# Attention and expert routing on one core: a pair's scores and its transposes each in one block, values in the scores' ring of PSUM tiles

## The chip, the cores and the metric

The kernel runs on one core of one Trainium2 chip. Its time is the device time of one execution in microseconds (us); the median of several runs counts. TensorE multiplies matrices into PSUM (8 banks), VectorE and ScalarE read PSUM, GpSimd issues the indirect DMAs, and SyncE issues all other DMAs.

## The reference

Causal attention over 4 batches of 12 heads (448 tokens, head dimension 64) gives 1792 rows of 768. They go through a layer of 8 experts. Routing is greedy over all pairs of token and expert in order of their logit, with at most 224 tokens for each expert; every token then passes through its expert's two matrices.

```python
scores = scale * np.matmul(q, k.transpose(0, 1, 3, 2))
scores = np.where(mask, -1e9, scores)
scores = scores - np.max(scores, axis=-1, keepdims=True)
attn = np.exp(scores)
attn = attn / (np.sum(attn, axis=-1, keepdims=True) + 1e-09)
x = np.matmul(attn, v)                 # rows of 12 heads x 64
...
flat = (x @ w_gate).flatten()
order = np.argsort(-flat)
for idx in order:
    tok, e = (int(idx) // E, int(idx) % E)
    if assigned[tok] >= 0 or counts[e] >= cap:
        continue
    assigned[tok] = e
    counts[e] += 1
...
for e in range(E):
    mask = assigned == e
    out[mask] = np.maximum(x[mask] @ w1[e], 0.0) @ w2[e]
```

## The kernel before

**Attention.** The 48 heads go in 24 pairs. A pair's two heads lie on partitions 0 to 63 and 64 to 127, so their score matmuls run side by side on two halves of TensorE's rows. The 448 queries are four blocks of 112; block i needs only the first 112 (i + 1) keys. `scores` (line 210) computes the blocks in sets, each set with a tile for each head: set (3,) has 448 columns, set (2, 0) has 336 + 112, set (1,) has 224. `mask` (VectorE) adds the causal mask, copies to SBUF and finds the row maximum; `exp` (ScalarE) exponentiates and sums. `transp` turns the 10 blocks of a head's probabilities on TensorE, in three groups of 4, 4 and 2, each in a tile; `keep_pt` copies each group to SBUF on ScalarE or VectorE. `av` multiplies by the values, with the two heads on two halves of TensorE's columns, and `xt_ev` copies the result (128 x 448, transposed) out. `rows_tr` and `rows_dve` turn it into rows, divide by the sums and put it into `xio`, which `store` writes to DRAM. Every four or two pairs, `logits_mm` and `logits_tr` compute gate logits.

**PSUM.** Three rings of tiles share the 8 banks: `s` (4, scores), `av` (1, values product) and `t` (3, everything else: groups of transposes, row turns, logits, and the last score set of pair 0). A ring hands its tiles out in order; a new user waits for whoever last read the tile.

**Order.** `plan` adds tasks for iterations n = 0 to 26. TensorE's tasks form one chain (`pe`, line 419), so its order is the order in which `plan` adds them; the other engines' orders come from a list scheduler (`Schedule.run`) that picks by priority and by durations written in the code. Among them copies of transposes stand above masks, and masks above exponentials. TensorE's order in an iteration is:

```python
self.score_set(n, (3,))
self.score_set(n, (2, 0))
self.turn(n - 1, 0)          # 10 transposes of one head
self.score_set(n, (1,))
self.turn(n - 1, 1)          # 10 of the other
self.rows_at(n - 3)
self.logits_back(n - 3)
self.values(n - 1)
self.logits(n - 2)
```

`extras` adds VectorE tasks of lowest priority that prepare the routing.

**Late rows.** `rows_at` serves only pairs below `LATE` = 12. The rows of the other pairs are turned later, by `late` (line 936), while the first routing decision runs on VectorE and TensorE. Each late pair is two half-pairs of two query blocks; a half-pair is divided into `xio` either by ScalarE (`rows_act`, four instructions) or by VectorE (`rows_dve`, one instruction). `PIECES` says after which pairs a part of `xio` is stored. Where TensorE has nothing to do in this stage, `filler` issues matmuls whose result nobody reads. The first gather of tokens (`gather`) needs the routing's list `idx` and all stores (`touch`, a small GpSimd write). Then the eight experts follow, each with its weights split in two parts.

Of the kernel before, what the change touches and what calls it, by code (L numbers as in the profile page):

```python
# [27 lines left out]
QO = (0, 112, 336, 672)  # L28
LATE = 12
PIECES = {14: 3, 17: 3, 20: 3, 22: 2, 23: 1}  # L30
WARM = 10
# [122 lines left out]
class Attention(Schedule):  # L154
    def __init__(self, ctx, tc, gc, keep, k, qk, vP, wgP, xd, L):
        super().__init__()
        self.tc, self.nc, self.k = tc, tc.nc, k
        self.qk, self.vP, self.xd, self.L = qk, vP, xd, L
        self.gc, self.keep = gc, keep
        self.ld = ctx.enter_context(tc.tile_pool(name="ld", bufs=4))  # L160
        self.wk = ctx.enter_context(tc.tile_pool(name="wk", bufs=4))
        self.cs = ctx.enter_context(tc.tile_pool(name="acs", bufs=1))
        self.ps = ctx.enter_context(tc.tile_pool(name="aps", bufs=1, space=PSUM))
        self.QK, self.V = {}, {}
        self.X, self.RS, self.XT, self.S, self.SM, self.PT, self.AV = {}, {}, {}, {}, {}, {}, {}
# [7 lines left out]
        t = self.ps.tile([C, 512], F32, name="t", bufs=3)  # L173
# [36 lines left out]
    def scores(self, pp, lst):  # L210
        ts = [self.ps.tile([C, 512], F32, name=n, bufs=b) for n, b in (("t", 3) if pp == 0 and 1 in lst else ("s", 4),) * 2]
        o = 0
# [27 lines left out]
    def transp(self, pp, sd, sg):  # L240
        P = self.SM[pp, sd][0]
        t = self.ps.tile([C, 512], F32, name="t", bufs=3)
# [22 lines left out]
    def av(self, pp, js):  # L265
        if 0 in js:
            self.AV[pp] = self.ps.tile([128, S], F32, name="av")
        for j in js:
            for sd in range(2):
                m = S - j * C  # L270
                self.nc.tensor.matmul(self.AV[pp][sd * 64:sd * 64 + 64, j * C:], self.V[2 * pp + sd][:, j, :],  # L271
                                      self.PT[pp, sd][:, KO[j]:KO[j] + m], start=j == 0, stop=j == 2)
# [7 lines left out]
    def xt_ev(self, e, pp):  # L280
        self.copy(e, self.XT[pp], self.AV.pop(pp))

# [14 lines left out]
    def rows_tr(self, pp):  # L297
        self.T[pp] = self.ps.tile([C, 512], F32, name="t", bufs=3)
        self.rows_mm(pp, self.T[pp])
# [16 lines left out]
    def rows_dve(self, pp, t, blocks=range(NC)):  # L316
        x, r = self.xslice(pp)
        s = slice(blocks[0], blocks[-1] + 1)
        self.nc.vector.tensor_tensor(x.rearrange("p i (s d) -> p i s d", s=2)[:, s],
                                     t.rearrange("p (i s d) -> p i s d", i=NC, s=2)[:, s], r[:, s], op=OP.mult)  # L320

# [4 lines left out]
    def logits_mm(self, b, half):  # L326
        p0, m = ((0, 4), (4, 2))[half]
        t = self.ps.tile([128, S], F32, name="t", bufs=3)
        for p in range(m):
# [4 lines left out]
    def logits_direct(self, pp):  # L334
        b, q = divmod(pp, 6)
        if q == 4:
            self.u = self.ps.tile([C, NC, 128], F32, name="t", bufs=3)
        for i in range(NC):
# [8 lines left out]
    def logits_tr(self, b, half):  # L347
        m = (4, 2)[half]
        self.u = self.ps.tile([C, NC, 128], F32, name="t", bufs=3)
        for i in range(NC):  # L350
# [26 lines left out]
    def plan(self, rt):  # L377
# [19 lines left out]
        for n in range(NP + 3):  # L397
            self.score_set(n, (3,))
            self.score_set(n, (2, 0))
            self.turn(n - 1, 0)  # L400
            self.score_set(n, (1,))
            self.turn(n - 1, 1)
            self.rows_at(n - 3)
# [19 lines left out]
    def score_set(self, pp, lst):  # L423
        if not 0 <= pp < NP:
            return
        add, pr = self.add, 5.5 - 0.1 * pp
        m = sum(C * (i + 1) for i in lst)

        def work():
            self.scores(pp, lst)  # L430
            if 1 in lst and pp in self.qfree:
                self.fire(self.qfree[pp])

        bank = "t" if pp == 0 and 1 in lst else "s"
        a = self.pe(m * 4 / 2400.0 + 0.01 * len(lst), work, [self.half0 if pp == 0 and 3 in lst else self.got[pp]] + (self.ring("s", 2) if bank == "s" else []), 1)
        free = []
        for sd in range(2):
            for i in lst:
                early = 0.5 if pp == sd == 0 else 0.0
                d = add("DVE", (0.27, 0.39, 0.51, 0.62)[i], lambda sd=sd, i=i: self.mask(pp, sd, i),  # L440
                        [a] + (self.ring("pt", 4 - sd) if i == 3 else []), pr + 0.25 + early)
                free.append(d)
                self.exps[pp, sd, i] = add("ACT", (0.385, 0.47, 0.56, 0.67)[i], lambda sd=sd, i=i: self.exp(pp, sd, i),
                                           [d], pr + early)
        if bank == "t":
            self.rings["t"] = [free[:1], free[1:]]
        else:
            self.rings.setdefault("s", []).append(free)
        if 1 in lst:
            self.rec[pp] = add("DVE", 0.25, lambda: self.recips(pp),  # L450
                               [self.exps[pp, sd, i] for sd in range(2) for i in range(NC)], pr - 0.3)

    def turn(self, pp, sd):
        if not 0 <= pp < NP:
            return
        pr = 5.5 - 0.1 * pp
        for sg, need in ((0, (3, 2, 1, 0)), (1, (3, 2, 1)), (2, (3, 2))):
            n = (4, 4, 2)[sg]
            a = self.pe(0.097 * n, lambda sg=sg: self.transp(pp, sd, sg),
                        [self.exps[pp, sd, i] for i in need] + self.ring("t", 3))  # L460
            dur = {"DVE": 0.31, "ACT": 0.24} if n == 2 else {"DVE": 0.545, "ACT": 0.43}
            c = self.add("ACT/DVE", dur, lambda e, sg=sg: self.keep_pt(e, pp, sd, sg), [a] + self.ring("av", 2), pr + 0.3)
            self.rings.setdefault("t", []).append([c])
            self.pts[pp, sd, sg] = c
        self.rings.setdefault("pt", []).append([a])

    def values(self, pp):
# [3 lines left out]
        for js, sg in (((0,), 0), ((1, 3), 1), ((2,), 2)):  # L471
# [18 lines left out]
        self.xts[pp] = self.add("ACT/DVE", {"ACT": 0.475, "DVE": 0.56}, ev, [a, self.xts.get(pp - 1)], pr + 0.3)  # L490
        self.rings.setdefault("xt", []).append([self.xts[pp]])

    def rows_at(self, pp):
# [3 lines left out]
        pr = 5.3 - 0.1 * pp  # L497
        t = self.pe(0.43, lambda: self.rows_tr(pp), [self.xts[pp]] + self.ring("t", 3))
        d = self.add("DVE", 0.61, lambda: self.rows_dve(pp, self.T.pop(pp)), [t, self.rec[pp]], pr + 0.3)
# [8 lines left out]
    def logits(self, pp):  # L508
        b, q = divmod(pp, 6)
        if pp in (NP - 2, NP - 1):  # L510
            free = self.ring("t", 3) if q == 4 else []
            self.lts = self.pe(0.4, lambda: self.logits_direct(pp), [self.xts[pp]] + free)
# [3 lines left out]
        if q not in (3, 5) or not 0 <= pp < NP:  # L516
# [4 lines left out]
        t = self.pe(0.77, lambda: self.logits_mm(b, half),  # L521
                    [self.xts[6 * b + p0 + u] for u in range(m)] + self.ring("t", 3), 3)
        c = self.add("ACT/DVE", {"ACT": 0.42, "DVE": 0.56}, lambda e: self.logits_cp(e, b, half), [t], pr + 0.3)
# [3 lines left out]
    def logits_back(self, pp):  # L527
# [8 lines left out]
        else:  # L536
            t = self.pe(0.43, lambda: self.logits_tr(b, half), [self.lts] + self.ring("t", 3))
        d = self.add("DVE", (1.1, 1.05)[half], lambda: self.logits_ev(b, half),
# [12 lines left out]
    def finish(self, rt):  # L551
        rt.early_count(self.G, self.ps.tile([128, S], F32, name="av"))

# [308 lines left out]
class Experts(Schedule):  # L862
# [73 lines left out]
    def late(self):  # L936
        at = self.at
        act, done = {}, []
        for n, pp in enumerate(range(LATE, NP)):
# [322 lines left out]
```

## Time and profile before

| | |
|---|---|
| median of 3 runs | 512.79 us (511.56 to 512.80) |
| the profiled execution | 514.21 us, span 512.3 us from the first to the last instruction |
| granted TensorE clock, mean | 0.999 |
| TensorE, VectorE, ScalarE busy | 496.0, 408.3, 281.6 us |
| pairs (scores to values) | about 6 to 184 us |
| first routing decision with late rows | about 185 to 204 us |
| experts | about 211 us to the end |

The profile is of one execution. Busy time is the sum of an engine's instructions; matmuls overlap, so their durations say less than the distance from one start to the next. A timeline row merges neighbouring instructions of one line and one engine: start, length from the first start to the last end, count, and in brackets the idle time before it and who ended it.

### The profile page before, as it was taken

Reading aid. Unit: us, or ns where it says so; the run is one execution under the profiler, and the core shown is the slowest. Engines: PE = TensorE matmul, PEld = TensorE weight load, DVE = VectorE, ACT = ScalarE, POOL = GpSimd, SP = SyncE. Lnnn points to the kernel's source line nnn. Section 1 sums busy time; section 2 is a strip of 40 time slices with the busy share of each in tenths; the row PEclk is TensorE's granted clock in tenths of the full one; section 3 lists DMA queues with packets and bytes.
Section 4 is the critical chain, followed back from the end, with each engine's and each line's share of the span. In section 5 each row is a group of like instructions: output and inputs, shape, how many; then the busy total and the mean of one; then the engine's idle time right before and its main releaser. Section 6 shows DMA issues by size and latency. Waiting matters only on the chain.

```text
span 512.3 us, 10576 instructions
## 1 busy us (share of the span) xinstructions
PE 496.0 (97%) x3909; PEld 407.5 (80%) x3909; DVE 408.3 (80%) x1330; ACT 281.6 (55%) x700; POOL 51.2 (10%) x86
## 2 busy tenths in 40 slices
PE   8999999999999988899999999999999999999995
PEld 5666566657666666698999999999989989999995
DVE  4898778877879966589999999999989787687720
ACT  5877678678778854136346624444444544754410
POOL 4000000000000010100030030120220510110102
PEclk9999999999999999999999999999999999999999
DMA  8923175118100007757877773584663975858101
GB/s 240 301 78 104 36 228 150 57 37 252 38 1 2 1 28 226 265 189 236 272 233 230 239 224 114 160 289 144 217 203 95 332 251 174 322 180 307 56 0 54
DMA packets 18883, 84.06 MB, mean 164 GB/s; under 512 B 2256, under 2 KB 4816, under 8 KB 18832
## 3 DMA queue, kind: packets, MB, share of 16 engines
q1 hardware_dynamic: 16160, 72.36, 43.8%
q0 software_dynamic: 2672, 11.04, 6.9%
q8 instruction: 30, 0.49, 0.4%
q14 instruction: 21, 0.17, 0.1%
HBM read 72.38 MB, written 11.01 MB: 163 GB/s over the span
## 4 chain that ended last, share of the span: by engine, by line
PE 79%; ACT 8%; DMA 5%; DVE 4%; issue 2%; POOL 0%; POOLq 0%; ACTq 0%; DVEq 0%
PE po L1196 25%; PE ph L1166 11%; PE av L271 10%; PE s L217 7%; PE ph L1170 6%; PE t L245 5%; ACT P L237 4%; DMA xio<-xd,idx 4%; PE ph L1161 3%; ACT PT L251 2%; PE rt L762 2%; PE ph L1132 2%; DVE Sm L227 2%; PE t L295 2%; DMA wr<-in_w 1%
## 5 line engine op out<-in xcount | busy, mean ns | idle before, releaser
L1091 ACT CAST wh<-wr 128x1536 fp32r<-128x1536 f32 x60 | 88.4, 1479 | 61.1 <-DMA wr<-in_w 59.0
L1097 DVE TENSOR_TENSOR wl<-wr,wh 128x512 fp32r<-128x512 f32 x180 | 115.8, 682 | 7.5 <-ACT wh L1091 7.4
L237 ACT ACTIVATE P<-Sm,mx 112x448 f32<-112x448 f32 (+2 forms) x192 | 99.5, 525 | 38.8 <-DVE mx L227 33.5
L1166 PE MATMUL ph<-xhl,wh 128*128 128x448 f32 x288 | 94.0, 380 | 0.0
L1170 PE MATMUL ph<-xhl,wl 128*128 128x224 f32 x336 | 89.7, 267 | 0.0
L227 DVE CUSTOM_DVE_ANT_0 Sm<-s,MK 112x448 f32<-112x448 f32 (+3 forms) x190 | 76.3, 443 | 8.6 <-PE s L217 8.6
L1196 PE MATMUL po<-wh,HH 128*112 128x384 f32 x256 | 68.3, 343 | 0.0
L1196 PE MATMUL po<-wl,HH 128*112 128x384 f32 x256 | 68.0, 341 | 0.0
L1196 PE MATMUL po<-wh,HL 128*112 128x384 f32 x256 | 67.2, 338 | 0.0
L1170 PEld LDWEIGHTS ph<-xhl,wl 128*128 128x128 f32 x336 | 64.2, 191 | 0.0
L217 PE MATMUL s<-raw 64*112 64x448 f32 (+3 forms) x380 | 58.1, 420 | 0.1
L1166 PEld LDWEIGHTS ph<-xhl,wh 128*128 128x128 f32 x288 | 54.2, 188 | 4.5 <-issue 0.3
L245 PE MATMUL t<-idf,P 112*112 112x112 f32 x480 | 56.3, 264 | 0.1
L245 PEld LDWEIGHTS t<-idf,P 112*112 112x112 f32 x480 | 45.8, 134 | 10.2 <-issue 7.1
L217 PEld LDWEIGHTS s<-raw 64*112 64x112 f32 x380 | 30.6, 172 | 29.1 <-issue 18.5
L271 PE MATMUL av<-PT,v 112*64 112x112 f32 (+3 forms) x384 | 52.2, 406 | 0.0
L1176 ACT ACTIVATE HH<-hs 128x224 fp32r<-128x224 f32 x48 | 18.8, 392 | 49.3 <-DVE hs L1180 47.8
L1196 PEld LDWEIGHTS po<-wh,HL 128*112 128x112 f32 x256 | 43.9, 174 | 0.3
L1196 PEld LDWEIGHTS po<-wl,HH 128*112 128x112 f32 x256 | 43.3, 175 | 0.3
L1196 PEld LDWEIGHTS po<-wh,HH 128*112 128x112 f32 x256 | 43.2, 175 | 0.2
L271 PEld LDWEIGHTS av<-PT,v 112*64 112x64 f32 x384 | 28.6, 136 | 17.6 <-issue 9.3
L1180 DVE TENSOR_REDUCE hs<-ph 128x224 f32<-128x448 f32 x48 | 29.8, 621 | 14.9 <-PE ph L1170 11.0
(160 smaller groups left out, 646.3 us busy)
## 6 DMA issues: line engine op xcount, KB each, us to landing
wr<-in_w SPq DMA_DIRECT2D x64, 768.0 KB, 5.2
raw<-in_qk SPq DMA_DIRECT2D x11, 896.0 KB, 6.5
v<-in_v SPq DMA_DIRECT2D x12, 448.0 KB, 3.7
xd<-xio SPq DMA_DIRECT2D x2, 1344.0 KB
xd<-xio SPq DMA_DIRECT2D x3, 672.0 KB, 4.2
raw<-in_qk SPq DMA_DIRECT2D x1, 448.0 KB
xd<-xio SPq DMA_DIRECT2D x1, 448.0 KB
xio<-xd,idx POOLq DMA_INDIRECT x16, 4.8
```

The lines of the kernel that those rows point to most:

```text
L217: self.nc.tensor.matmul(ts[sd][:, o:o + m], q[:, 0, i * C:i * C + C], q[:, 1, :m], start=True, stop=True)
L227: self.nc.vector.tensor_tensor_reduce(Sm[:, QO[i]:QO[i] + m], self.S.pop((pp, sd, i)), self.MK[:, S - m:], -0.125, 3.0e38, OP.add, OP.min, ...
L237: self.nc.scalar.activation(P[:, s], Sm[:, s], AF.Exp, bias=mx[:, i:i + 1], scale=-1.0, accum_out=self.RS[b][:, pr, sd * NC + i:sd * NC + ...
L245: self.nc.tensor.transpose(t[:, o + (i - j) * C:o + (i - j) * C + C], P[:, QO[i] + j * C:QO[i] + j * C + C], self.k["idf"][:C, :C])
L271: self.nc.tensor.matmul(self.AV[pp][sd * 64:sd * 64 + 64, j * C:], self.V[2 * pp + sd][:, j, :], self.PT[pp, sd][:, KO[j]:KO[j] + m], star ...
L1091: self.nc.scalar.copy(hi, self.R[p, c])
L1097: self.nc.vector.tensor_sub(lo[:, s], self.R[p, c][:, s], hi[:, s].bitcast(F32))
L1166: nc.tensor.matmul(t[:, :2 * CAP], hi[:, s], x[:, d].rearrange("p z t -> p (z t)"), start=d == 0, stop=False)
L1170: nc.tensor.matmul(t[:, :CAP], lo[:, s], x[:, d, 0], start=False, stop=d == 5)
L1176: self.nc.scalar.activation(self.HH[p][:, f], self.P[p, f][:, :CAP], AF.Relu)
L1180: self.nc.vector.tensor_reduce(t, self.P[p, f][:, :2 * CAP].rearrange("p (z t) -> p t z", z=2), axis=AX.X, op=OP.add)
L1196: self.nc.tensor.matmul(self.T[p, "o", u][z][:, :384], a[p][:, f, u * C:u * C + C], w[:, o:o + 384], start=f == 0 and n == 0, stop=f == 7 ...
```

## The change

All scores of a pair come in one block, with set (1,) first from pair 1 on, in two tiles of the ring `t`, which now has 4 tiles. Then come the 20 transposes of the pair before, group by group with both heads in turn; the first group of each head is copied by ScalarE only. The values product takes a tile of the ring `s`; the ring `av` is gone. `LATE` is 10, so pairs 10 and 11 become late pairs and get a store of their own (`PIECES[11] = 2`), and their transposed rows a tile of their own (`xt_room`). `rows_dve`, where it serves a half-pair, issues one instruction for each query block, two in all.

```diff
-LATE = 12
-PIECES = {14: 3, 17: 3, 20: 3, 22: 2, 23: 1}
+LATE = 10
+PIECES = {11: 2, 14: 3, 17: 3, 20: 3, 22: 2, 23: 1}
...
-        ts = [self.ps.tile([C, 512], F32, name=n, bufs=b) for n, b in (("t", 3) if pp == 0 and 1 in lst else ("s", 4),) * 2]
+        ts = [self.ps.tile([C, 512], F32, name=n, bufs=b) for n, b in (("t", 4) if 1 in lst else ("s", 4),) * 2]
...
-            self.AV[pp] = self.ps.tile([128, S], F32, name="av")
+            self.AV[pp] = self.ps.tile([128, 512], F32, name="s", bufs=4)
...
-        s = slice(blocks[0], blocks[-1] + 1)
-        self.nc.vector.tensor_tensor(x.rearrange("p i (s d) -> p i s d", s=2)[:, s],
-                                     t.rearrange("p (i s d) -> p i s d", i=NC, s=2)[:, s], r[:, s], op=OP.mult)
+        for s in (slice(0, NC),) if len(blocks) == NC else (slice(i, i + 1) for i in blocks):
+            self.nc.vector.tensor_tensor(x.rearrange("p i (s d) -> p i s d", s=2)[:, s],
+                                         t.rearrange("p (i s d) -> p i s d", i=NC, s=2)[:, s], r[:, s], op=OP.mult)
...
-            self.score_set(n, (3,))
-            self.score_set(n, (2, 0))
-            self.turn(n - 1, 0)
-            self.score_set(n, (1,))
-            self.turn(n - 1, 1)
+            for lst in ((3,), (2, 0), (1,)) if n == 0 else ((1,), (3,), (2, 0)):
+                self.score_set(n, lst)
+            self.turns(n - 1)
...
-        a = self.pe(m * 4 / 2400.0 + 0.01 * len(lst), work, [self.half0 if pp == 0 and 3 in lst else self.got[pp]] + (self.ring("s", 2) if bank == "s" else []), 1)
+        bank = "t" if 1 in lst else "s"
+        ring = self.ring("s", 2) if bank == "s" else self.ring("t", 4) + self.ring("t", 3)
+        a = self.pe(m * 4 / 2400.0 + 0.01 * len(lst), work, [self.half0 if pp == 0 and 3 in lst else self.got[pp]] + ring, 1)
...
-    def turn(self, pp, sd):
+    def turns(self, pp):
...
         for sg, need in ((0, (3, 2, 1, 0)), (1, (3, 2, 1)), (2, (3, 2))):
             n = (4, 4, 2)[sg]
+            for sd in range(2):
+                a = self.pe(0.097 * n, lambda sg=sg, sd=sd: self.transp(pp, sd, sg),
+                            [self.exps[pp, sd, i] for i in need] + self.ring("t", 4))
+                dur = {"DVE": 0.31, "ACT": 0.24} if n == 2 else {"DVE": 0.545, "ACT": 0.43}
+                one = sg == 0
+                c = self.add("ACT" if one else "ACT/DVE", dur["ACT"] if one else dur,
+                             lambda e="ACT", sg=sg, sd=sd: self.keep_pt(e, pp, sd, sg), [a] + self.ring("av", 2), pr + 0.3)
...
-            a = self.pe(m * 4 / 2400.0 + 0.02, work, deps + (self.ring("xt", 1) if 0 in js else []), 2)
+            a = self.pe(m * 4 / 2400.0 + 0.02, work, deps + (self.ring("s", 4) if 0 in js else []), 2)
...
-            act[n] = [self.add("ACT/DVE", {"ACT": 0.89, "DVE": 0.35}, lambda e, pp=pp, box=box, i=i: self.late_rows(e, pp, box["t"], i),
+            act[n] = [self.add("ACT/DVE", {"ACT": 0.89, "DVE": 0.41}, lambda e, pp=pp, box=box, i=i: self.late_rows(e, pp, box["t"], i),
```

## Rows read from the trace of the kernel before

**Rows 1.** Windows: busy us and instructions of PE, PEld, DVE, ACT, POOL; clock; DMA.

```profile
16.00:184.00 168.00, 166.53 (x1307) 107.83 (x1308) 139.99 (x554) 125.90 (x432) 0.97 (x4) 1.00 0.30 91
...
160.00:180.00 20.00, 19.95 (x160) 13.88 (x159) 18.60 (x74) 15.88 (x57) 0.00 (x0) 1.00 0.00 2
```

**Rows 2.** Timeline of PE, an iteration without a row turn.

```profile
163.89 1.77 PE L217 MATMUL s<-raw 64*112 64x448 f32 x12
165.59 1.17 PE L245 MATMUL t<-idf,P 112*112 112x112 f32 x10
166.69 0.64 PE L217 MATMUL s<-raw 64*112 64x224 f32 x4
167.26 1.17 PE L245 MATMUL t<-idf,P 112*112 112x112 f32 x10
168.36 2.22 PE L271 MATMUL av<-PT,v 112*64 112x448 f32 x16
170.51 1.77 PE L217 MATMUL s<-raw 64*112 64x448 f32 x12
```

**Rows 3.** Timeline of PE, an iteration with a row turn.

```profile
29.68 1.77 PE L217 MATMUL s<-raw 64*112 64x448 f32 x12
...
33.05 1.17 PE L245 MATMUL t<-idf,P 112*112 112x112 f32 x10
34.27 0.65 PE L295 MATMUL t<-idf,xt 128*112 128x128 f32 x4
34.85 2.11 PE L271 MATMUL av<-PT,v 112*64 112x448 f32 x16
36.88 1.77 PE L217 MATMUL s<-raw 64*112 64x448 f32 x12
```

**Rows 4.** Chain that ended last, 0 to 60 us: start, length, what.

```profile
25.91 0.54 PE t L245 x4
```

**Rows 5.** Timeline of PE, first score block of pair 1.

```profile
7.70 2.98 PE L217 MATMUL s<-raw 64*112 64x448 f32 x12
```

**Rows 6.** Timelines of ACT and DVE, 160 to 174 us.

```profile
161.28 0.97 ACT L251 COPY PT<-t 112x448 f32<-112x448 f32 x2 [0.59 <-PE t L245]
...
165.79 0.67 ACT L237 ACTIVATE P<-Sm,mx 112x448 f32<-112x448 f32 x1 [0.77 <-DVE mx L227]
...
170.62 0.62 DVE L253 COPY xt<-av 128x448 f32<-128x448 f32 x1
```

**Rows 7.** Row division on DVE: busy and mean ns (first); min/median/max ns (second).

```profile
L319 DVE TENSOR_TENSOR xio<-t,rs 112x512 f32<-112x512 f32 x10 | 6.9, 691 | 0.6
...
L319 DVE TENSOR_TENSOR xio<-po,rs x11: 410/417/425, 187.6 to 197.3; 112x256 f32<-112x256 f32 x11
```

**Rows 8.** Timeline of DVE, first routing decision.

```profile
190.85 0.42 DVE L319 TENSOR_TENSOR xio<-po,rs 112x256 f32<-112x256 f32 x1 [0.45 <-ACT xio L313]
...
192.10 0.42 DVE L319 TENSOR_TENSOR xio<-po,rs 112x256 f32<-112x256 f32 x1
192.44 0.17 DVE L745 SCALAR_TENSOR_TENSOR kr<-rt,kr 112x16 int16<-112x16 f32 x1
...
194.38 0.76 DVE L319 TENSOR_TENSOR xio<-po,rs 112x256 f32<-112x256 f32 x2 [0.89 <-ACT xio L313]
```

**Rows 9.** Timeline of ACT, first routing decision.

```profile
186.36 5.28 ACT L313 ACTIVATE xio<-po,rs 112x64 f32<-112x64 f32 x24 [0.80 <-PE po L295]
192.61 1.74 ACT L313 ACTIVATE xio<-po,rs 112x64 f32<-112x64 f32 x8 [0.97 <-DVE kr L745]
195.18 4.20 ACT L313 ACTIVATE xio<-po,rs 112x64 f32<-112x64 f32 x20 [0.82 <-DVE xio L319]
```

**Rows 10.** What the first gather waits for: stores' landing, GpSimd's touch, the list.

```profile
DMA to landing us min/median/max: 4.0/4.2/4.3
...
203.62 0.09 POOL L1101 MEMSET xio<- 1x1 f32 x1 [5.49 <-DMA xd<-xio]
...
203.63 0.16 DVE L847 CAST idx<-rt 112x2 int32<-112x2 f32 x1 [0.40 <-PE rt L844]
```

More of the change, by code (lines that the diff above doesn't have):

```diff
@@ L172, in __init__ @@
         nc.vector.memset(zero, 0.0)
-        t = self.ps.tile([C, 512], F32, name="t", bufs=3)
+        t = self.ps.tile([C, 512], F32, name="t", bufs=4)
         for _ in range(WARM):
@@ L241, in transp @@
         P = self.SM[pp, sd][0]
-        t = self.ps.tile([C, 512], F32, name="t", bufs=3)
+        t = self.ps.tile([C, 512], F32, name="t", bufs=4)
         for j, o in (((0, 0),), ((1, 0), (3, 336)), ((2, 0),))[sg]:
@@ L270, in av @@
                 m = S - j * C
-                self.nc.tensor.matmul(self.AV[pp][sd * 64:sd * 64 + 64, j * C:], self.V[2 * pp + sd][:, j, :],
+                self.nc.tensor.matmul(self.AV[pp][sd * 64:sd * 64 + 64, j * C:S], self.V[2 * pp + sd][:, j, :],
                                       self.PT[pp, sd][:, KO[j]:KO[j] + m], start=j == 0, stop=j == 2)
@@ L280, in xt_ev @@
     def xt_ev(self, e, pp):
-        self.copy(e, self.XT[pp], self.AV.pop(pp))
+        self.copy(e, self.XT[pp], self.AV.pop(pp)[:, :S])
     def xt_room(self, pp):
@@ L297, in rows_tr @@
     def rows_tr(self, pp):
-        self.T[pp] = self.ps.tile([C, 512], F32, name="t", bufs=3)
+        self.T[pp] = self.ps.tile([C, 512], F32, name="t", bufs=4)
         self.rows_mm(pp, self.T[pp])
@@ L327, in logits_mm @@
         p0, m = ((0, 4), (4, 2))[half]
-        t = self.ps.tile([128, S], F32, name="t", bufs=3)
+        t = self.ps.tile([128, S], F32, name="t", bufs=4)
         for p in range(m):
@@ L336, in logits_direct @@
         if q == 4:
-            self.u = self.ps.tile([C, NC, 128], F32, name="t", bufs=3)
+            self.u = self.ps.tile([C, NC, 128], F32, name="t", bufs=4)
         for i in range(NC):
@@ L348, in logits_tr @@
         m = (4, 2)[half]
-        self.u = self.ps.tile([C, NC, 128], F32, name="t", bufs=3)
+        self.u = self.ps.tile([C, NC, 128], F32, name="t", bufs=4)
         for i in range(NC):
@@ L427, in score_set @@
         m = sum(C * (i + 1) for i in lst)
+        last = lst == ((1,) if pp == 0 else (2, 0))
         def work():
             self.scores(pp, lst)
-            if 1 in lst and pp in self.qfree:
+            if last and pp in self.qfree:
                 self.fire(self.qfree[pp])
-        bank = "t" if pp == 0 and 1 in lst else "s"
-        a = self.pe(m * 4 / 2400.0 + 0.01 * len(lst), work, [self.half0 if pp == 0 and 3 in lst else self.got[pp]] + (self.ring("s", 2) if bank == "s" else []), 1)
+        bank = "t" if 1 in lst else "s"
+        ring = self.ring("s", 2) if bank == "s" else self.ring("t", 4) + self.ring("t", 3)
+        a = self.pe(m * 4 / 2400.0 + 0.01 * len(lst), work, [self.half0 if pp == 0 and 3 in lst else self.got[pp]] + ring, 1)
         free = []
@@ L440, in score_set @@
                 d = add("DVE", (0.27, 0.39, 0.51, 0.62)[i], lambda sd=sd, i=i: self.mask(pp, sd, i),
-                        [a] + (self.ring("pt", 4 - sd) if i == 3 else []), pr + 0.25 + early)
+                        [a] + (self.ring("pt", 4 - sd) if (pp, sd, i) in ((0, sd, 3), (pp, sd, 1)) else []), pr + 0.25 + early)
                 free.append(d)
@@ L445, in score_set @@
         if bank == "t":
-            self.rings["t"] = [free[:1], free[1:]]
+            self.rings.setdefault("t", []).extend([free[:1], free[1:]])
         else:
             self.rings.setdefault("s", []).append(free)
-        if 1 in lst:
+        if last:
             self.rec[pp] = add("DVE", 0.25, lambda: self.recips(pp),
                                [self.exps[pp, sd, i] for sd in range(2) for i in range(NC)], pr - 0.3)
-    def turn(self, pp, sd):
+    def turns(self, pp):
         if not 0 <= pp < NP:
@@ L458, in turn @@
             n = (4, 4, 2)[sg]
[L459 to L465, printed above, removed]
+            for sd in range(2):
[5 more added lines that the diff above has]
+                             lambda e="ACT", sg=sg, sd=sd: self.keep_pt(e, pp, sd, sg), [a] + self.ring("av", 2), pr + 0.3)
+                self.rings.setdefault("t", []).append([c])
+                self.pts[pp, sd, sg] = c
+                if sg == 2:
+                    self.rings.setdefault("pt", []).append([a])
     def values(self, pp):
@@ L490, in values @@
         self.xts[pp] = self.add("ACT/DVE", {"ACT": 0.475, "DVE": 0.56}, ev, [a, self.xts.get(pp - 1)], pr + 0.3)
-        self.rings.setdefault("xt", []).append([self.xts[pp]])
+        self.rings.setdefault("s", []).append([self.xts[pp]])
     def rows_at(self, pp):
@@ L497, in rows_at @@
         pr = 5.3 - 0.1 * pp
-        t = self.pe(0.43, lambda: self.rows_tr(pp), [self.xts[pp]] + self.ring("t", 3))
+        t = self.pe(0.43, lambda: self.rows_tr(pp), [self.xts[pp]] + self.ring("t", 4))
         d = self.add("DVE", 0.61, lambda: self.rows_dve(pp, self.T.pop(pp)), [t, self.rec[pp]], pr + 0.3)
@@ L510, in logits @@
         if pp in (NP - 2, NP - 1):
-            free = self.ring("t", 3) if q == 4 else []
+            free = self.ring("t", 4) if q == 4 else []
             self.lts = self.pe(0.4, lambda: self.logits_direct(pp), [self.xts[pp]] + free)
@@ L521, in logits @@
         t = self.pe(0.77, lambda: self.logits_mm(b, half),
-                    [self.xts[6 * b + p0 + u] for u in range(m)] + self.ring("t", 3), 3)
+                    [self.xts[6 * b + p0 + u] for u in range(m)] + self.ring("t", 4), 3)
         c = self.add("ACT/DVE", {"ACT": 0.42, "DVE": 0.56}, lambda e: self.logits_cp(e, b, half), [t], pr + 0.3)
@@ L536, in logits_back @@
         else:
-            t = self.pe(0.43, lambda: self.logits_tr(b, half), [self.lts] + self.ring("t", 3))
+            t = self.pe(0.43, lambda: self.logits_tr(b, half), [self.lts] + self.ring("t", 4))
         d = self.add("DVE", (1.1, 1.05)[half], lambda: self.logits_ev(b, half),
@@ L551, in finish @@
     def finish(self, rt):
-        rt.early_count(self.G, self.ps.tile([128, S], F32, name="av"))
+        rt.early_count(self.G, self.ps.tile([128, S], F32, name="t", bufs=4))
 def constants(nc, cs):
```

## The prediction

> **What bounds the kernel now.** I read the windows first, then TensorE's timeline, then the chain of waits, and last the timelines of the stage behind the pairs. From 16 to 184 us, where the head pairs are worked off, TensorE is busy 166.5 of 168 us at a granted clock of 1.00 (the 2.4 GHz level), VectorE 140.0, ScalarE 125.9 [rows 1]. So the pace there is TensorE's, and the reader should see in its timeline what a pair costs. From the start of one block to the start of the next, an iteration without a row turn takes 1.70 (scores, 12 matmuls), 1.10 (10 transposes), 0.57 (scores, 4), 1.10 (transposes), 2.15 (values): 6.62 us [rows 2]. One with a row turn takes 7.20: the row block is 0.58, and the transposes ahead of it last 1.22 instead of 1.10 because the row turn waits for a copy; the values then take 2.03 [rows 3].
>
> Behind the pairs, from 185 to 204 us, the first routing decision runs on VectorE and TensorE in turn, and the late rows lie between its steps [rows 8, 9]. Its end and the last store's landing release the first gather within 0.2 us of each other [rows 10]. After the gather TensorE is full again to the end, so I take what is won or lost before the gather as won or lost in the total.
>
> **The parts of the change.** *Two blocks fewer per iteration.* What does a block cost beyond its columns? The two score blocks stream 896 and 224 columns per head in 1.70 and 0.57 us: (1.70 - 0.57) / 672 = 1.68 ns per column, so 224 columns are 0.38 and 0.19 is left over. For transposes, 10 take 1.10 and the chain shows 4 in 0.54 [rows 2, 4]: 0.093 each, 0.17 left over. The change puts all scores in one block and all 20 transposes in one, so an iteration loses one of each leftover: 0.36 us. Iterations 1 to 23 hold both scores and transposes: 23 x 0.36 = 8.3 us. This is the term I trust most, since it is TensorE's own time and not a wait.
>
> *The start.* The first score block of pair 1 lasts 2.98 us instead of 1.77 [rows 2, 5], because it waits for masks of pair 0 to free the score banks. The four matmuls that now come ahead of it use a ring with free banks, so their 0.38 us falls into that wait. I take 0.4.
>
> *Two row turns leave the pairs.* LATE goes from 12 to 10, so iterations 13 and 14 become iterations without rows: 2 x (7.20 - 6.62) = 1.2 us.
>
> *The waits.* Four transpose tiles replace three, but six groups now come in a row instead of three and three, and the first two are evicted by ScalarE alone. A group of four passes in 0.37 us, so the sixth, which needs the second one's bank, could start 4 x 0.37 + 0.19 = 1.68 us after the first did. ScalarE sees the first after 0.54 [rows 4], and its two copies take 0.97 [rows 6], some 1.05 with the hand-overs: 1.59, 0.09 to spare. But an exponential already running lasts up to 0.67 [rows 6], so the sixth group waits between 0 and 0.58 us; with the exponential met anywhere in its length, 0.25 on average. Now a row iteration loses 0.29 at this place (1.22 less ten transposes' 0.93, [rows 3]) and one without rows about 0.13 before its values (2.15 against 2.03, [rows 2, 3]), which then no longer hang on the copy just made. So 10 x (0.25 - 0.29) + 13 x (0.25 - 0.13) = +1.2 us. The bounds are -4.6 (no wait left: 10 x 0.29 + 13 x 0.13) and +8.7 (0.58 each time, less the 4.6 lost now). I take +1.2.
>
> *The values product in the scores' ring.* It adds a wait: the second tile of scores 2 and 0 of the next pair reuses the bank of the values product and needs its copy. Between the end of the values and that matmul lie the score blocks of 224 and 448 columns, 0.38 + 0.75 us, plus the 0.17 us of the changeover: 1.3 us. The copy takes about 0.6 and can find an instruction of about 0.6 in front of it [rows 6]. So it is just hidden, price 0; uncovered it delays TensorE by 0.1 to 0.3, and masks and exponentials of that pair stand behind it. The other moved score tiles reuse banks that masks freed several microseconds before. The load that waits on a pair's last score fires at about the same place, and the DMA engines are 30% busy in this stage [rows 1]: nothing.
>
> *The late stage.* It gets four more half-pairs on top of 24 (11 on VectorE, 13 on ScalarE at 5.28 / 6 = 0.88 us [rows 7, 9]). One on VectorE takes 0.34 from start to start [rows 8]. Split by block it becomes two instructions of 128 elements, which this trace does not have; 512 elements last 691 ns and 256 about 417 [rows 7], 1.07 ns per element, so 128 last about 0.28 and pass in 0.20, two in 0.40 (an estimate; the bounds are 0.34 as now and 0.68, if each costs as much as one of 256). With two of the four on VectorE that is 2 x 0.40 + 11 x 0.06 = 1.5 us more of VectorE in the routing's steps; ScalarE's two, 1.8 us, fit into the 1.79 us that it waits between its three runs [rows 9]. TensorE's 8 more transposes take the place of its filler matmuls. Against this, VectorE twice stands still on a ScalarE write of the output rows, 0.45 and 0.89 us [rows 8], with the routing's next step queued behind it. The two write different columns; a write of two blocks spans the columns of other pairs in between, one of a single block doesn't. So I read these two waits as an artefact of the span, which the split removes: -1.3 us. There is one store more on SP, ahead of the others (448 KB, landing 4.2 us after issue [rows 10]), and rows of pairs 18 on must wait for it, about halfway through the stage. Bounds: -1.3 (waits go, the rest is hidden) and +3.5 (all four on VectorE and the split, 2.3, plus 1.2 for the store). I take +0.5.
>
> The sum: -8.3 - 0.4 - 1.2 + 1.2 + 0.5 = -8.2 us. The profiled execution took 514.2 us (span 512.3), so 506.0; the median of the runs shown is 1.4 lower, 512.8, so 504.6.
>
> **Rivals.** *B, eviction becomes the bound.* From 160 to 180 us VectorE and ScalarE together are already busy 86% of their time, VectorE 93% [rows 1]. An iteration of 6.26 us instead of 6.62 asks for 91%. If 86% is what they can do, the iterations without rows stay at 6.62 and only the ten with rows gain: 3.6 + 1.2 + 0.4 - 0.5 = 4.7 us, a median of 508.1. Against it: that stretch holds routing preparation of lowest priority, which fills idle time, and ScalarE is 79% busy and can take copies over. The Trainium skill, TensorEngine Tiling (Array Packing), PSUM Bottleneck, warns of just this: array tiling speeds TensorE, but not the emptying of PSUM, which may become the bottleneck. By that rule the time is this rival's; the trace bears it out only in VectorE's 93%, not in any stall of TensorE.
>
> *C, the late stage gives it back.* All of the upper bound, +3.5, instead of +0.5: 507.6. For it: 28 half-pairs in a stage whose VectorE steps set the gather. Against it: the end of the rows and the end of the routing now meet by chance [rows 10], so a delay of one alone costs little at first.
>
> *D, the waits go as well.* -4.6 instead of +1.2 for TensorE's waits and -1.3 instead of +0.5 in the late stage, 7.6 us less: 497.0. For it: one more bank, and the planner may place the copies where no exponential runs. Against it: ScalarE is 75% busy over the stage [rows 1].
>
> *E, slower.* In the burst of 20 transposes ScalarE has one whole exponential more ahead of the first copy. Then the sixth group waits 0.67 us longer in each iteration, 23 x 0.67 = 15.4 us, a median of 520. It decides from (8.2 + 1.5) / 23 = 0.42 us of wait per iteration beyond the 0.25. Against it: copies outrank exponentials in the planner's order, and the orders on the engines come from its own durations, which agree with the trace (0.43 planned for a copy; two take 0.97 with the second's tail).
>
> **How the numbers follow.** I give the forecast 0.51 (its own range 501 to 507.5), B 0.19, C 0.12, D 0.08, E 0.07, and 0.03 to new waits of just the size that cancels the gain. A difference under 0.3% (1.5 us) can't be told from no change here. Slower is E, 0.07; no change 0.04, with B's far end; faster the rest, 0.89. The range of 499.5 to 510.5 takes in the forecast, B and C with their bounds and leaves out most of D, E and little else.
>
> **What would show it.** In the changed profile the score block should have 16 matmuls in about 2.07 us from start to start, the transposes 20 in about 2.03, an iteration without rows about 6.4 and one with rows about 6.8; the direct logits should end near 176 us instead of 185. The two waits of VectorE on ScalarE's row writes should be gone, the single-block instruction should last 0.28 us, and the first gather should come about 8 us earlier, with everything behind it shifted alike. The forecast is wrong if TensorE's weight loads wait for ScalarE copies by 0.3 us or more in the transpose burst, if iterations without rows stay at 6.6, or if the stretch from the direct logits to the gather grows by more than 2 us.

## The result and the profile after

The changed kernel takes 506.0 us (median of 4 runs, 503.98 to 508.38) against 512.79 (4 runs, 511.56 to 514.82): a ratio of 0.9864, 95% interval 0.9830 to 0.9898. The forecast was 504.6. In a second set of runs beside the experiments it took 505.4, ratio 0.9851 (0.9833 to 0.9869). So the total came out as forecast to 1.4 us, but two of its terms were off by 2 to 3 us, in opposite directions. One run of the experiments (535.9 us, of the old order with new rings and copies free) fell into a slower state of the chip and is left out of its median.

The profiled execution took 505.19 us with a span of 503.5. TensorE's timeline has the shape that was drawn ahead: 16 score matmuls, then 20 transposes, then values. Without a row turn (the same view as [rows 2]):

```profile
114.27 0.64 PE L217 MATMUL t<-raw 64*112 64x224 f32 x4
114.74 1.68 PE L217 MATMUL s<-raw 64*112 64x448 f32 x12
116.35 2.13 PE L245 MATMUL t<-idf,P 112*112 112x112 f32 x20
118.40 2.11 PE L271 MATMUL s<-PT,v 112*64 112x448 f32 x16
120.44 0.64 PE L217 MATMUL t<-raw 64*112 64x224 f32 x4
```

From start to start: scores 2.08 (two blocks took 2.27), transposes 2.05 (2.20), values 2.04 (2.15), together 6.17 us instead of 6.62. With a row turn (the same view as [rows 3]):

```profile
29.00 0.64 PE L217 MATMUL t<-raw 64*112 64x224 f32 x4
29.47 1.68 PE L217 MATMUL s<-raw 64*112 64x448 f32 x12
31.08 2.13 PE L245 MATMUL t<-idf,P 112*112 112x112 f32 x20
33.19 0.65 PE L295 MATMUL t<-idf,xt 128*112 128x128 f32 x4
33.77 2.11 PE L271 MATMUL s<-PT,v 112*64 112x448 f32 x16
35.80 0.64 PE L217 MATMUL t<-raw 64*112 64x224 f32 x4
```

Scores 2.08, transposes 2.11 with the wait for a copy in front of the row turn, row turn 0.58, values 2.03: 6.80 instead of 7.20. The start gained little. The first two iterations end at 15.74 instead of 15.86, since the transposes of pair 0 now stand where its exponentials are not yet done (timeline, idle time before a row in brackets):

```profile
10.80 0.59 PE L245 MATMUL t<-idf,P 112*112 112x112 f32 x4
11.59 0.31 PE L245 MATMUL t<-idf,P 112*112 112x112 f32 x1 [0.20 <-ACT P L237]
12.06 1.71 PE L245 MATMUL t<-idf,P 112*112 112x112 f32 x15 [0.16 <-ACT P L237]
...
15.74 0.64 PE L217 MATMUL t<-raw 64*112 64x224 f32 x4
```

In all, the direct logits start at 172.67 us instead of 183.32: 10.65 us earlier. But the first gather starts only 7.84 us earlier, at 196.55 instead of 204.39. The stage between them has grown by 2.8 us. VectorE's timeline in it (the same views as [rows 8, 10]):

```profile
180.62 0.49 DVE L319 TENSOR_TENSOR xio<-po,rs 112x128 f32<-112x128 f32 x2 [0.46 <-ACT xio L313]
181.44 0.49 DVE L319 TENSOR_TENSOR xio<-po,rs 112x128 f32<-112x128 f32 x2 [0.33 <-ACT xio L313]
...
184.29 0.89 DVE L319 TENSOR_TENSOR xio<-po,rs 112x128 f32<-112x128 f32 x4 [0.92 <-ACT xio L313]
...
190.44 0.49 DVE L319 TENSOR_TENSOR xio<-po,rs 112x128 f32<-112x128 f32 x2 [0.73 <-ACT xio L313]
...
194.81 0.16 DVE L851 CAST idx<-rt 112x2 int32<-112x2 f32 x1 [0.40 <-PE rt L848]
```

The waits on ScalarE's row writes that the split was to remove are all there, four of them, 2.4 us instead of 1.3 (a second profile of the same kernel puts only three of them, 1.7 us, down to ScalarE). And the chain that ended last (start, length, what) no longer goes through the routing's list but through the last rows and their store:

```profile
187.01 3.40 ACT xio L313 x16
...
190.44 0.50 DVE xio L319 x2
190.94 0.02 SPq L324
...
190.99 4.56 DMA xd<-xio
...
195.77 0.09 POOL xio L1105
195.86 0.69 issue
196.55 1.03 POOL xio L1110
```

From the gather to the end it is 306.95 us instead of 307.91; two executions of the changed kernel differ by 0.6 there, so I make nothing of it.

Eviction, the copying of results out of PSUM by VectorE and ScalarE, did not become the bound, though it came nearer. Windows of the changed kernel (columns as in [rows 1]):

```profile
20.00:40.00 20.00, 20.00 (x166) 13.53 (x166) 16.91 (x76) 18.37 (x64) 0.00 (x0) 1.00 0.46 144
...
150.00:170.00 20.00, 19.98 (x172) 13.77 (x168) 17.93 (x75) 17.14 (x58) 0.00 (x0) 1.00 0.00 1
```

VectorE and ScalarE together are busy 88% in both and TensorE misses nothing; ScalarE is 17 to 18 of 20 us busy where it was 16 [rows 1].

### The profile page after: what moved, and what is told of

Same layout as the page of the kernel before. It is cut to its first block, busy times and chain, and to the rows that moved or that the text cites. A ratio compares the mean times of both kernels' runs of the same rounds, so it can differ in the third digit from the quotient of the medians.

```text
span 503.5 us, 10599 instructions
## 1 busy us (share of the span) xinstructions
PE 487.4 (97%) x3907; PEld 404.7 (80%) x3907; DVE 394.3 (78%) x1308; ACT 292.5 (58%) x741; POOL 50.8 (10%) x86
## 4 chain that ended last, share of the span: by engine, by line
PE 84%; DMA 6%; ACT 3%; POOL 2%; DVE 2%; issue 2%; POOLq 0%; DVEq 0%; ACTq 0%; SPq 0%
PE po L1200 25%; PE ph L1170 11%; PE t L245 10%; PE s L271 10%; PE s L217 7%; PE ph L1174 6%; DMA xio<-xd,idx 4%; PE ph L1165 3%; PE t L217 2%; PE rt L766 2%; ACT xio L313 2%; PE ph L1136 2%; DMA wr<-in_w 1%; PE t L295 1%; PE t L330 1%
## 5 line engine op out<-in xcount | busy, mean ns | idle before, releaser
L237 ACT ACTIVATE P<-Sm,mx 112x224 f32<-112x224 f32 (+2 forms) x192 | 99.1, 523 | 22.7 <-DVE mx L227 22.7
L227 DVE CUSTOM_DVE_ANT_0 Sm<-s,MK 112x448 f32<-112x448 f32 (+1 forms) x144 | 59.6, 464 | 6.5 <-POOL iof L579 5.8
L245 PE MATMUL t<-idf,P 112*112 112x112 f32 x480 | 52.6, 262 | 0.4 <-ACT P L237 0.4
L271 PE MATMUL s<-PT,v 112*64 112x448 f32 (+3 forms) x384 | 50.6, 406 | 0.0
L251 ACT COPY PT<-t 112x448 f32<-112x448 f32 (+1 forms) x109 | 42.7, 465 | 1.2 <-PE t L245 1.1
L217 PE MATMUL s<-raw 64*112 64x112 f32 (+2 forms) x288 | 41.4, 415 | 0.1
L271 PEld LDWEIGHTS s<-PT,v 112*64 112x64 f32 x384 | 23.2, 136 | 21.3 <-issue 9.8
```

The costliest lines, as they stand in the source:

```text
L217: self.nc.tensor.matmul(ts[sd][:, o:o + m], q[:, 0, i * C:i * C + C], q[:, 1, :m], start=True, stop=True)
L227: self.nc.vector.tensor_tensor_reduce(Sm[:, QO[i]:QO[i] + m], self.S.pop((pp, sd, i)), self.MK[:, S - m:], -0.125, 3.0e38, OP.add, OP.min, ...
L237: self.nc.scalar.activation(P[:, s], Sm[:, s], AF.Exp, bias=mx[:, i:i + 1], scale=-1.0, accum_out=self.RS[b][:, pr, sd * NC + i:sd * NC + ...
L251: self.nc.scalar.copy(out, x)
```

## The experiments

What follows compares positions in the traces, because they are steadier than totals. All in us from the span's start; the list is the cast of the first expert's indices. Each ratio is against runs of the kernel before in the same set, whose medians lie between 512.8 and 515.2; medians of different sets are not to be compared to the last microsecond.

| kernel | median, ratio to before (95%) | direct logits | list | first gather |
|---|---|---|---|---|
| before | 512.8 | 183.32 | 203.63 | 204.39 |
| changed | 506.0, 0.9864 (0.9830 to 0.9898) | 172.67 | 194.81 | 196.55 |
| changed, again | 505.4, 0.9851 (0.9833 to 0.9869) | 172.51 | 194.82 | 196.06 |
| old order, new rings | 527.1, 1.0298 (1.0247 to 1.0349) | 196.79 | 218.64 | 219.97 |
| the same, copies free | 529.7, 1.0341 (1.0239 to 1.0443) | 199.09 | 221.11 | 222.19 |
| new order, old rings | 528.9, 1.0309 (1.0257 to 1.0360) | 193.90 | 215.77 | 217.20 |
| three blocks | 512.4, 0.9999 (0.9962 to 1.0036) | 181.65 | 203.48 | 204.82 |
| copies free | 504.9, 0.9816 (0.9735 to 0.9897) | 172.97 | 195.08 | 195.60 |
| late part alone | 513.3, 0.9996 (0.9957 to 1.0035) | 181.63 | 203.50 | 204.73 |
| LATE 12 | 503.2, 0.9813 (0.9778 to 0.9848) | 173.62 | 194.73 | 195.48 |
| LATE 12, no split | 503.4, 0.9782 (0.9701 to 0.9862) | 173.08 | 193.76 | 194.48 |
| LATE 12, own banks | 502.3, 0.9742 (0.9662 to 0.9822) | 173.19 | 192.21 | 194.57 |
| LATE 12, own banks, no split | 504.7, 0.9816 (0.9761 to 0.9871) | 174.48 | 192.86 | 195.11 |
| LATE 14, own banks, no split | 502.1, 0.9784 (0.9730 to 0.9838) | 174.99 | 193.43 | 193.87 |

**The changed kernel again**, to have it on the chip of the first experiments.

> The changed kernel once more, beside the others: 506 us, ratio about 0.986. Pairs end (start of the direct logits) at 172.7 us, first gather at 196.6 us.

It did what was expected; its two profiles differ by 0.16 us at the direct logits and by 0.5 at the gather.

**The order undone, the rings kept.**

```diff
-            for lst in ((3,), (2, 0), (1,)) if n == 0 else ((1,), (3,), (2, 0)):
-                self.score_set(n, lst)
-            self.turns(n - 1)
+            self.score_set(n, (3,))
+            self.score_set(n, (2, 0))
+            self.turns(n - 1, 0)
+            self.score_set(n, (1,))
+            self.turns(n - 1, 1)
...
```

> The order of before (two score blocks and two transpose blocks in each iteration) with the new rings (four transpose tiles, values in the scores' ring). If the gain of the pairs is that of two blocks fewer, 0.36 us each iteration comes back: pairs end near 181 us, total about 514. Rival, that the fourth transpose tile made the gain: pairs end under 176 us, total under 509.

Pairs end 24 us later than in the changed kernel and 13 us later than before. Neither theory had this. TensorE's timeline shows the place, in nearly every iteration:

```profile
36.07 0.98 PE L245 MATMUL t<-idf,P 112*112 112x112 f32 x8
37.52 0.40 PE L245 MATMUL t<-idf,P 112*112 112x112 f32 x2 [0.47 <-ACT PT L251]
```

Score set 1 holds two of the four transpose tiles between the two bursts, so the second burst has two left for its three groups, and the third waits for a copy. Is it the binding of copies to ScalarE that makes the copy late? In the next kernel every copy is free for either engine.

```diff
-                one = sg == 0
+                one = False
```

> The order of before with the new rings, and all copies of transposes free for either engine, as before. If the loss of the old order with the new rings came from the copies bound to ScalarE, each behind exponentials: under 516. Rival, that the old order itself doesn't fit the new rings (the second transposes need a bank of the first, the score set 1 holds two in between): 520 or more.

```profile
27.60 0.98 PE L245 MATMUL t<-idf,P 112*112 112x112 f32 x8
29.07 0.41 PE L245 MATMUL t<-idf,P 112*112 112x112 f32 x2 [0.49 <-ACT PT L251]
...
28.51 0.51 ACT L251 COPY PT<-t 112x448 f32<-112x448 f32 x1
...
29.17 0.38 DVE L227 CUSTOM_DVE_ANT_0 Sm<-t,MK 112x224 f32<-112x224 f32 x1
```

The same wait at the same place (0.3 to 0.5 us, now for a copy by either engine); the rival holds. The third group starts right behind the copy of a group of its own burst (28.51) and before VectorE has begun to read the score set's tiles (29.17). So it didn't take the tile next in order, as the section on the kernel before says of the rings, but the first that came free. The old order and the new rings don't fit.

**The rings undone, the order kept.**

```diff
-        ... for n, b in (("t", 4) if 1 in lst else ("s", 4),) * 2]
+        ... for n, b in (("t", 3) if pp == 0 and 1 in lst else ("s", 4),) * 2]
...
-            self.AV[pp] = self.ps.tile([128, 512], F32, name="s", bufs=4)
+            self.AV[pp] = self.ps.tile([128, 512], F32, name="av")
...
```

> The new order with the rings of before (three transpose tiles, one tile for the values, all score sets in the scores' ring). If the blocks alone make the gain: pairs end within 2 us of the changed kernel's 172.7, total 506 to 508. Rival, that the burst of six groups needs the fourth tile: each iteration waits 0.3 us or more in its transposes, pairs end after 179 us, total 512 or more.

```profile
16.34 2.45 PE L217 MATMUL s<-raw 64*112 64x224 f32 x16
18.72 1.36 PE L245 MATMUL t<-idf,P 112*112 112x112 f32 x12
20.32 1.02 PE L245 MATMUL t<-idf,P 112*112 112x112 f32 x8 [0.24 <-ACT PT L251]
21.27 2.11 PE L271 MATMUL av<-PT,v 112*64 112x448 f32 x16
```

The rival holds: three tiles stop the burst after 12 transposes (20 take 2.55 us to the next start instead of 2.05), and six score tiles in a ring of four stop the score block (2.38 instead of 2.08). The blocks alone cost 3.1%, the rings alone 3.0 to 3.4%; together they gain. (Both kernels also have the late part of the change, which by itself moves the total by nothing, as shown below.)

**One block more**, with the transposes together: score set 1 goes ahead of the values product.

```diff
-            for lst in ((3,), (2, 0), (1,)) if n == 0 else ((1,), (3,), (2, 0)):
+            for lst in ((3,), (2, 0), (1,)) if n == 0 else ((3,), (2, 0)):
                 self.score_set(n, lst)
             self.turns(n - 1)
             self.rows_at(n - 3)
             self.logits_back(n - 3)
+            if n:
+                self.score_set(n, (1,))
...
```

> The changed kernel with score set 1 of a pair moved from the head of the score block to a block of its own just ahead of the values product; the 20 transposes stay together. One block more in each of 23 iterations. If a block costs what its row left over, 0.19 us: pairs end 4.4 us later, at 177 us, total about 510. Rival, that the place of the masks and exponentials matters more than the count of blocks: pairs end after 181 us, total 514 or more.

Pairs end 9.1 us later, between the two. The timeline tells the two apart:

```profile
34.06 0.65 PE L295 MATMUL t<-idf,xt 128*112 128x128 f32 x4
34.64 0.64 PE L217 MATMUL t<-raw 64*112 64x224 f32 x4
35.20 2.11 PE L271 MATMUL s<-PT,v 112*64 112x448 f32 x16
37.24 1.83 PE L217 MATMUL s<-raw 64*112 64x448 f32 x12
...
120.49 2.36 PE L245 MATMUL t<-idf,P 112*112 112x112 f32 x20
122.78 1.18 PE L217 MATMUL t<-raw 64*112 64x224 f32 x4
123.90 2.11 PE L271 MATMUL s<-PT,v 112*64 112x448 f32 x16
```

Where a row turn lies in between, the block lasts 0.56 us to the next start, 0.18 more than its columns, and the whole iteration (30.19 to 37.24) is 7.05 us, 0.25 longer than the changed kernel's: near the price of a block. Where none lies in between, the block lasts 0.8 to 1.1 us, because it needs tiles that the burst has just filled: its weight loads wait for ScalarE's copies, up to 0.3 us each time. So the block's price is right, and the place of the tiles' users costs about as much again (9.1 us instead of 4.4).

**Copies free**, in the changed kernel (the edit shown above).

> The changed kernel with the first group's copies free for either engine. If binding them to ScalarE is needed: new waits of TensorE in the transpose burst, pairs end after 175 us, total 508 or more. Rival, that the order of the blocks alone carries the gain: pairs end at 172 to 173.5 us, total 504 to 506.5.

The rival's numbers come: pairs end at 172.97. The binding to ScalarE isn't needed and is worth 0.3 to 0.5 us at most. That the order alone carries the gain doesn't follow: with the old rings it lost 3.1%.

**The late part alone**, on the kernel before: `LATE` 10, its store, and the split.

```diff
-LATE = 12
-PIECES = {14: 3, 17: 3, 20: 3, 22: 2, 23: 1}
+LATE = 10
+PIECES = {11: 2, 14: 3, 17: 3, 20: 3, 22: 2, 23: 1}
...
-        s = slice(blocks[0], blocks[-1] + 1)
+        for s in (slice(0, NC),) if len(blocks) == NC else (slice(i, i + 1) for i in blocks):
...
```

> The kernel before with only the late part of the change: LATE 10, its store, and the split. From the runs so far: pairs 1.1 us shorter, the stage behind them 2.6 us longer, total about 514.5, 1.5 us slower than before. Rival, the forecast: pairs 1.2 us shorter, stage 0.5 us longer, total 512.

No difference in time: the total lies between the two. The direct logits come 1.7 us earlier, more than either expected; the stretch to the gather takes 23.10 us instead of 21.07, 2.0 longer, nearer the 2.6 than the forecast's 0.5.

**LATE back to 12**, all else as changed:

```diff
-LATE = 10
-PIECES = {11: 2, 14: 3, 17: 3, 20: 3, 22: 2, 23: 1}
+LATE = 12
+PIECES = {14: 3, 17: 3, 20: 3, 22: 2, 23: 1}
```

> LATE back to 12, all else as changed. If the late stage was lengthened by its four more half-pairs: pairs end 1.3 us later (two row turns), the stretch from direct logits to gather falls from 23.9 to about 21 us, total about 504.5. Rival, that the split into blocks lengthened it: the stretch stays above 23 us, total about 507.

And without the split as well:

```diff
-        for s in (slice(0, NC),) if len(blocks) == NC else (slice(i, i + 1) for i in blocks):
+        s = slice(blocks[0], blocks[-1] + 1)
...
```

> LATE 12 and the late rows on VectorE in one instruction for a half-pair, as before; the rest as changed. If the split only costs VectorE time: the stretch from direct logits to gather falls from 21.9 us (LATE 12 with split) to about 21.1 as before, total 502.4. Rival, the forecast's reading that the split removes waits on ScalarE's row writes: these waits grow and the stretch is 22.5 us or more, total 504.

With `LATE` 12 the logits start 1.1 us later than in the changed kernel's second profile and the stretch to the gather falls from 23.6 to 21.9; without the split to 21.4, with the list 0.43 us earlier after the logits (20.68 instead of 21.11). Both parts lengthened the stage: the four half-pairs by 1.7 us, the split by 0.4; why 21.4 us are left and not the 21.07 of the kernel before is not explained, and the totals, 503.2 and 503.4, don't tell the two kernels apart. The forecast's reading of the split is out: without it VectorE's waits on ScalarE are 1.3 us, with it 1.7.

**Own banks.** Each half-pair gets a tile, which is a PSUM bank, of its own instead of both halves of a pair sharing one. A bank is then free again once its own half is read, where before both halves had to be.

```diff
-                if i == 0:
-                    box["t"] = self.bank(n % 4)
-                at.rows_mm(pp, box["t"], (i,))
+                if i % 2 == 0:
+                    box[i // 2] = self.bank((2 * n + i // 2) % 4)
+                at.rows_mm(pp, box[i // 2], (i,))
...
```

> LATE 12 with the split, and each late half-pair turned into a PSUM bank of its own instead of both halves of a pair in one bank (four banks, so two pairs in flight instead of four). If VectorE and ScalarE wait for each other because the two halves share a bank: VectorE's waits on ScalarE's row writes (1.7 us in three) fall under 0.3 us, the stretch from direct logits to gather under 21 us, total about 502. Rival, that the writes into the row tile make the waits: they stay above 1.2 us, total 503 or more.

Who waited for whom between 173 and 200 us (total, times, longest), first with a bank for each pair, then with a bank for each half-pair, where the first line and every other wait between the two engines' row writes is gone:

```profile
DVE xio L319 <- ACT xio L313: 1.7, 3, 0.9
```

```profile
ACT xio L313 <- PE po L295: 1.8, 4, 0.6
```

Both engines still write the same row tile in turns; in the middle of a run of ScalarE's, VectorE now starts without a wait (timelines of this kernel):

```profile
176.02 5.07 ACT L313 ACTIVATE xio<-po,rs 112x64 f32<-112x64 f32 x24 [0.58 <-PE po L295]
...
177.83 0.48 DVE L319 TENSOR_TENSOR xio<-po,rs 112x128 f32<-112x128 f32 x2
```

The list is ready 19.02 us after the logits' start instead of 21.11. So the shared bank made the waits (or the tile that fills it: these runs don't tell the two apart), and not the row tile. That all of the 2.1 us on the list comes from them is not shown: the waits were 1.7, ScalarE now also has 14 half-pairs instead of 13, and two pairs are in flight instead of four. But the gather starts only 0.5 us earlier in its stretch (21.38, where under 21 was expected): it now waits for the last store, 1.6 us behind the list. Taking the split out as well, by the edit shown above:

> LATE 12, own banks for the late half-pairs and one VectorE instruction for a half-pair. If the waits came from the shared bank alone, the split is now only cost: the list of the first gather is ready 0.5 us earlier than with the split, but the last store's landing sets the gather, so total 501.5 to 502.5. Rival, that the split also frees something: 503 or more.

The list comes 18.38 us after the logits, 0.64 earlier, and with two-block writes VectorE doesn't wait for ScalarE's row writes either, so the split is only cost. The total, 504.7, is above the expectation, where the rival had it; the last section says where its profiled execution lost time.

**LATE 14.** With fewer late rows the last store should come earlier. The edit, on the kernel with own banks and no split:

```diff
-LATE = 12
-PIECES = {14: 3, 17: 3, 20: 3, 22: 2, 23: 1}
+LATE = 14
+PIECES = {15: 2, 17: 2, 20: 3, 22: 2, 23: 1}
```

> As the kernel with LATE 12, own banks and no split, but with LATE 14: two more row turns among the pairs (+1.2 us there) and four half-pairs fewer behind them. If the late stage is still stretched by its half-pairs by 0.45 us each, it gains 1.8 us: total 501. Rival, that the routing chain itself is now the bound: no gain behind the pairs, total 503 or more.

The stretch to the gather falls to 18.88 us, 1.75 less than with `LATE` 12 (20.63), as expected. But the list stays where it was after the logits (18.44 us instead of 18.38), so four half-pairs no longer stretch the routing; it is the store that lands 2 us earlier. Against the changed kernel the stretch is 4.7 us shorter, for 2.5 us more of pairs; list and store now meet again. At 502.1 us it and the other kernels with own banks or `LATE` 12 lie 1 to 4 us under the changed kernel; their intervals overlap, so which of them is best stays open. All beat the kernel before (their intervals lie below 1), and the one with `LATE` 14 has the earliest gather.

## Why the prediction was right, and where it was wrong

- **Two blocks fewer, 8.3 us: right.** Scores and transposes save 0.19 and 0.15 us in an iteration without rows (forecast 0.36 together), and the block put back cost 0.25 where nothing else interfered.
- **The start, 0.4 us: wrong.** Together with its two blocks, 0.76 was to be gained up to the end of iteration 1; it was 0.12. The scores of pair 1 did take less, but the prediction didn't ask what is late next: the exponentials of pair 0, for which its transposes then wait.
- **Two row turns, 1.2 us: right**, 1.1 (`LATE` 12 against 10, with the new order; 1.7 with the old one).
- **The waits, +1.2 us: wrong in sign, about -2.** Added up over TensorE's timelines from the end of iteration 1 to the direct logits, scores take 4.0 us less, transposes 4.2, values 1.2 and row turns 1.2. A block fewer in each of 22 iterations explains 3.3 to 3.7 us of the transposes (0.15 to 0.17 each). What is left of transposes and values, 1.6 to 2.0 us, is waits that are gone: the 0.11 in front of the values, and a little in front of the row turn, where 0.25 (2.11 less 20 x 0.093) still stands. The mechanism was right. Where ScalarE starts an exponential 0.23 us into the burst (150.04 us), the last two transposes, the sixth group, wait for its second copy (timelines of the changed kernel; PEld is TensorE's loading of weights):

```profile
150.27 0.65 ACT L237 ACTIVATE P<-Sm,mx 112x448 f32<-112x448 f32 x1
...
150.92 1.43 ACT L251 COPY PT<-t 112x448 f32<-112x448 f32 x3
...
151.91 0.19 PEld L245 LDWEIGHTS t<-idf,P 112*112 112x112 f32 x2 [0.16 <-ACT PT L251]
```

This happens in 4 of the 21 bursts between 24 and 165 us, which last 0.08 to 0.27 us longer for it. In the other 17 the exponential starts 0.03 to 0.05 us into the burst and is over soon after the first group, as here in the burst at 116.35:

```profile
116.38 0.66 ACT L237 ACTIVATE P<-Sm,mx 112x448 f32<-112x448 f32 x1
...
117.03 1.88 ACT L251 COPY PT<-t 112x448 f32<-112x448 f32 x5
```

The copies then start 0.68 to 0.71 us into the burst and the burst waits for none of them. So the step that failed is the exponential "met anywhere in its length": the engines' orders are planned, and it is met at nearly the same place each time: only its last 0.14 to 0.17 us (0.68 to 0.71 less 0.54) stand in the copies' way. Rival D had thought of this. The room for it was also larger: bursts grow only where the first copy starts later than about 0.73 us (an estimate: 0.81 costs 0.08 and 1.00 costs 0.27), 0.19 behind the 0.54 instead of 0.09.

- **The values product in the scores' ring, 0: right.** The score block of 12 passes in 1.60 or 1.61 us in all but one of the iterations from 2 on (1.71 at 154.8 us).
- **The late stage, +0.5 us: wrong, +2.5 to +2.8.** The term that failed is the -1.3 us for the split. VectorE's waits do not come from the span that is written but from the bank that the two halves share: with banks of their own they vanish, split or not. The size of the split instruction was right (280 ns, and two pass in 0.40 us). By the prediction's own sign, a stretch to the gather that grows by more than 2 us, this part of the forecast was wrong, though the total came out. What was left of the sum, half-pairs and split, measured 1.7 and 0.4 us. The store also became the gather's last condition, as rival C had it; "a delay of one alone costs little at first" didn't help, since both were delayed.

So -10.65 us up to the direct logits (forecast -8.7) and +2.8 behind them (+0.5) gave -7.85 at the gather, where -8.2 was forecast. That the total came so near is partly luck: two errors cancelled.

Of the rivals, B's premise, that VectorE and ScalarE can do no more than 86%, didn't hold: they reach 88%, and iterations without rows fell to 6.17 us. The Trainium skill, TensorEngine Tiling (Array Packing), PSUM Bottleneck, says that tiling speeds up TensorE but not the emptying of PSUM, which may become the bottleneck; the trace of the changed kernel doesn't bear that out here, with TensorE busy 20.00 and 19.98 of 20 us. E's mechanism, copies too late for the burst, is what the order alone and the rings alone run into.

The Trainium skill, PSUM — Partial Sum Buffer, PSUM bank collisions raise a hardware error, says that two engines must not use one bank on the same partitions at once, two readers included. The traces fit it: with a shared bank the program lets VectorE wait until ScalarE has read its half, 0.3 to 0.9 us each time, and with separate banks it doesn't. No run here lets both read one bank at once.

## What to carry to other kernels

Count what a block of like matmuls leaves over beside its columns, and gather them, but only together with the tiles that the longer burst needs: here either half of the change alone lost 3%. When two engines wait for each other over data that don't overlap, look at the bank that they read before the region that they write. And price a stage by its last two conditions, not by one: the saving on the list was worth little until the store came earlier too.

## What the runs showed of the hardware

A wait of TensorE can cost more than its length. In the kernel with `LATE` 12, own banks and no split, the profiled execution stood idle for 2.5 us around 414 us, waiting for an expert's gather, and then ran on at a granted clock of 0.50 (the 1.2 GHz level) after 1.00 (windows, columns as in [rows 1]):

```profile
412.00:414.00 2.00, 1.57 (x12) 1.03 (x10) 1.63 (x4) 1.39 (x2) 0.00 (x0) 1.00 0.87 280
414.00:416.00 2.00, 0.00 (x0) 0.00 (x0) 0.00 (x0) 0.00 (x0) 0.00 (x0) 1.00 0.67 221
416.00:418.00 2.00, 1.90 (x11) 1.86 (x12) 0.89 (x2) 1.46 (x4) 0.00 (x0) 0.72 0.02 9
418.00:420.00 2.00, 2.00 (x8) 1.90 (x7) 2.00 (x5) 2.00 (x2) 0.00 (x0) 0.50 0.00 0
```

In those last 2 us it began 8 matmuls where the same line begins 13 or 14 at a clock of 1.00 (422 to 430 us). In the changed kernel's profile TensorE missed 0.9 us between 400 and 420 and the clock stayed at 1.00. The four runs of this kernel reach from 502.5 to 507.8 us; whether such a fall of the clock makes all of that spread was not shown. It is one reason to compare stages by their positions.
